# Query and key groups transposed by the DMA engines instead of VectorE

## The chip, the cores and the metric

One core of one Trainium2 chip runs the whole program. The metric is the device time of the program in microseconds (us), the median over runs.

## The reference

Chunked attention (chunks of 64 tokens, each attending only to itself), then a two-layer network with a leaky ReLU. Inputs and output are float32.

```python
batch, n_heads, seq, head_dim = (8, 8, 576, 64)      # q, k, v
chunk = 64
scores = scale * np.matmul(q_c, k_c.transpose(0, 1, 2, 4, 3))     # per chunk of 64
scores = scores - np.max(scores, axis=-1, keepdims=True)
attn = np.exp(scores)
attn = attn / (np.sum(attn, axis=-1, keepdims=True) + 1e-09)
out = np.matmul(attn, v_c)
...
x = out.transpose(0, 2, 1, 3).reshape(4608, 512)
h = x @ w_in                       # 512 x 2048
g = np.maximum(0.01 * h, h)
return g @ w_out                   # 2048 x 512
```

## The kernel before

The 4608 tokens are cut into 36 groups of 128 tokens (two chunks of 64, all eight heads). Each group u goes through the attention stages and leaves 128 columns of `xT`; the network runs over 19 blocks of 128 or 256 tokens. Everything is in float16 on TensorE, with float32 sums.

The order of all instructions is written out by the kernel itself. After a written prologue (`FRONT`), the network's matmuls form a list `chunks`; each of them advances a counter `step` by one (by a half in the last two blocks). Attention stages are events with a due step, `at(step, ...)`, and each is issued when the counter reaches it. `T[u]` is the step at which the scores of group u are due; the distances between neighbours are in the list `SPACE` (3.5 to 10.5 steps). Every engine then executes its own part of that one order, in order.

The stages of a group that matter here:

- loading: `load_qk(u)` (L73) reads q and k of the group by natural rows (token on the partition), float32 in DRAM to float16 in SBUF, by DMAs that GpSimd (POOL) issues (L91), into the tiles `q_in` and `k_in` with five buffers each. For groups 14 to 35 another loader is used: `load_qk_batch` (L95, DMAs at L105) brings one batch of 576 tokens by 16 DMAs, in a layout in which 32x32 blocks can be transposed within 32 partitions (`q_d`, `k_d`).
- transposing: the scores need the head dimension on the partition. For groups below `UD = 14`, TensorE transposes q and k against an identity (`stage_tq`, `stage_tk`, L674) into PSUM (`qp`, `kp`), then VectorE copies q into `QZ` (`stage_q`, L701, two copies a group) and ScalarE copies k into `KT` (`stage_k`, L712). From group 14 on VectorE transposes 32x32 blocks straight into `QZ` (`stage_dq`, L724, two a group) and `KT` (`stage_dk`, L732), 7 steps ahead of the scores.
- scores: `stage_s` (L742), eight matmuls into `Sp`. Then the row maximum `mx` (L751), from group 14 on its negative `nb` (L764) and eight exponentials with row sums on ScalarE (L772); before that a subtraction (L755) and one exponential (L785). The sum with its small addend is `ze` (L796), its reciprocal `zi` (L798), the normalised weights `en` (L803), which VectorE computes for groups below 10 and POOL for the others.
- `stage_d` (L825): one DMA transpose on SyncE's (SP) queue turns `en` into `et`. `stage_v` (L836) multiplies it with v; ScalarE copies the result into `xT` (L850).

v comes by DMAs that POOL issues (L112); one half of a batch's buffer is reloaded when the group that last read it is done. SP's queue also carries all stores of the output (L282 and others).

Below, "group 16" is u = 16, counted from 0, so the tenth group is u = 9.

Of the kernel before, what the change touches and what calls it, by code (L numbers as in the profile page):

```python
# [8 lines left out]
FP16 = mybir.dt.float16  # L9
# [7 lines left out]
def kernel(  # L17
# [9 lines left out]
    nc = tc.nc  # L27

    B, H, S, D = q.shape
# [3 lines left out]
    CH = 64  # L33
# [4 lines left out]
    NQZ = 3  # L38
    NVB = 2
    NIN = 5  # L40
    PAIRED = range(1, 4)
    UD = 14
    LEAD = 5
    UE = 5
    UX = 14
    G = 2 * CH

    NU = n_tok // G
# [9 lines left out]
    sbp = ctx.enter_context(tc.tile_pool(name="k_sb", bufs=1))  # L58
# [5 lines left out]
    QZ = [sbp.tile([128, 4, 2, 2, CH], FP16, name=f"QZ{i}") for i in range(NQZ)]  # L64
# [8 lines left out]
    def load_qk(u):  # L73

        both = []
        for name, src in (("q_in", q), ("k_in", k)):
            if u in PAIRED:
                t = sbp.tile([CH, H, 2, D], FP16, name=name, tag=name + "2", bufs=len(PAIRED))
            else:
                t = sbp.tile([128, H, D], FP16, name=name, tag=name, bufs=NIN)  # L80
            r0, r1 = u * G, (u + 1) * G
            cut = min(-(-r0 // S) * S, r1) if r0 % S else r1
            for a, z in ((r0, cut), (cut, r1)):
                if a < z:
# [7 lines left out]
            both.append(t)  # L92
        qk[u] = tuple(both)

    def load_qk_batch(b, i):  # L95

        if i == 0:
            qkd[b] = tuple(
                sbp.tile([128, 2, 2, S // 32, 32], FP16, name=name, tag=name, bufs=2) for name in ("q_d", "k_d")
            )  # L100
        i, n = divmod(i, 2)
        m, s, dh = i // 4, i // 2 % 2, i % 2
        t, src = qkd[b][n], (q, k)[n]
        p0, h0 = s * 64 + dh * 32, 4 * m + 2 * s
        nc.gpsimd.dma_start(  # L105
            out=t[p0:p0 + 32, m, :, :, :].rearrange("p h b d -> p (h b) d"),
            in_=src[b, h0:h0 + 2, :, dh * 32:dh * 32 + 32].rearrange("h (b t) d -> t (h b) d", t=32),
        )

    def load_v(b):  # L110
        for m in range(2):
            nc.gpsimd.dma_start(  # L112
                out=VB[b % NVB][m * CH:(m + 1) * CH, :, :, m * CH:(m + 1) * CH].rearrange("p h c d -> p (h c) d"),
                in_=v[b, m * H // 2:(m + 1) * H // 2].rearrange("h (c j) d -> j (h c) d", j=CH),
            )
# [21 lines left out]
    for eng, name, src in ((nc.sync, "q_f", q), (nc.scalar, "k_f", k)):  # L137
        t = sbp.tile([128, H, D], FP32, name=name, tag="sh", bufs=2)
# [11 lines left out]
    LOADS = (  # L150
        "g2 g1 g3 v0 Q0 Q1 g4 Q2 Q3 g5 P0 P1 P3 P2 g6 v1 g7 g8 "
    )
    LOADERS = {"g": load_qk, "v": load_v, "Q": load_w_in_quarter, "P": load_w_out_quarter, "D": lambda b: [load_qk_batch(b, i) for i in range(16)]}
    ident = sbp.tile([128, 128], FP16, name="ident")
    for n, what in enumerate(LOADS.split()):
        LOADERS[what[0]](int(what[1:]))
        if n == 0:
# [181 lines left out]
    def w_in_sum(n):  # L339
        h = HF // 2 * 128  # L340
        w = w_inT.rearrange("p (k t) (s h f) -> p k h t s f", k=2, s=2, h=2)
        b11, b12, b21, b22 = w[:, 0, 0], w[:, 0, 1], w[:, 1, 0], w[:, 1, 1]
        x, y = {1: (b12, b11), 2: (b22, None), 3: (b22, b12), 4: (b21, None)}[n]
        if y is None:
            y = WS[{2: 0, 4: 1}[n]]
        to = sbp.tile([128, 2, 2, h], FP16, name=f"WS{n}", tag="q_d" if n % 2 else "k_d", bufs=2, padded_shape=[128, 2, 2, 576])
        for s in range(2):
            nc.vector.tensor_tensor(out=to[:, :, s], in0=x[:, :, s], in1=y[:, :, s], op=ALU.subtract)
        WS.append(to)
# [306 lines left out]
    D_D = 3  # L656
# [35 lines left out]
    def stage_q(u, s, act=0):  # L692
        part = slice(s * CH, (s + 1) * CH)
        to, of = QZ[u % NQZ][part, :, :, s, :], QP[u][part]
        if u in PAIRED:
            to = to.rearrange("p i e (j r) -> p (i e) r j", r=2)
# [4 lines left out]
            nc.vector.tensor_copy(out=to, in_=of)  # L701

    def stage_k(u, dve=0):
        KT[u] = sbp.tile([128, 4, 2, CH], FP16, name="KT", tag="KT", bufs=3)
# [9 lines left out]
    def cuts(u):  # L714
        r0, r1 = u * G, (u + 1) * G
        cut = min(-(-r0 // S) * S, r1) if r0 % S else r1
        return [(a // S, a % S, (a - r0) // CH, (z - a) // CH) for a, z in ((r0, cut), (cut, r1)) if a < z]

    flat = lambda t: t.rearrange("p m h b d -> p (m h) (b d)")

    def stage_dq(u, s):
        qz = QZ[u % NQZ]
        for b, at, e0, n in cuts(u):
            nc.vector.transpose(  # L724
                out=qz[s * CH:(s + 1) * CH, :, e0:e0 + n, s, :],
                in_=flat(qkd[b][0])[s * CH:(s + 1) * CH, :, at:at + n * CH].rearrange("p h (e t) -> p h e t", e=n),
            )

    def stage_dk(u):
        KT[u] = sbp.tile([128, 4, 2, CH], FP16, name="KT", tag="KT", bufs=3)  # L730
        for b, at, e0, n in cuts(u):
            nc.vector.transpose(  # L732
                out=KT[u][:, :, e0:e0 + n, :],
                in_=flat(qkd[b][1])[:, :, at:at + n * CH].rearrange("p h (e t) -> p h e t", e=n),
            )

    def stage_s(u):
        qz, kt = QZ[u % NQZ], KT.pop(u)
# [91 lines left out]
    def stage_v(u):  # L830
        et = ET.pop(u)
        xp = psp.tile([128, NT, 2, CH], FP32, name="xp", tag="ox", bufs=1)
        for e in range(2):
            b, c = divmod(2 * u + e, NCH)
            for t in range(NT):
                nc.tensor.matmul(  # L836
                    out=xp[:, t, e, :],
                    lhsT=VB[b % NVB][:, t, c, :],
                    rhs=et[:, t // 2, e, t % 2, :] if u < UD else et[:, t % 2, e, t // 2, :],
                    start=True,  # L840
                    stop=True,
                )
            if c == NCH - 1 and b + NVB < B:
                load_v(b + NVB)
        XP[u] = xp
# [47 lines left out]
    def zero_act(i):  # L893
# [23 lines left out]
        "I": identity, "st": store_held, "nb": stage_nb, "f": stage_f, "dq": stage_dq, "dk": stage_dk, "D": load_qk_batch,  # L917
# [17 lines left out]
    for what in FRONT.split():  # L935
        name = what.rstrip("0123456789.")
# [8 lines left out]
    VO = [-1.5, 1.0, 0.5, 0.0, 1.0, -0.5, 2.5, 1.5, 0.0, 1.5, 6, 1.5, -0.5, 1.5, -0.5, 1.5, 1.5, -2.5, -0.5, 1.0, 4.5, 0.5, 0.0, 1.0, 3.0, 3.5, -0.5, -1.0, -6.0, -3.0]  # L945
    O_T = 6
    O_P = 4.0
    O_Q = 7.0
    O_R = 1.25
    O_M = 0  # L950
    O_X = 1.5
    O_F = 1.5
# [6 lines left out]
    O_L = 4.0  # L959
    O_W = -13  # L960
    O_Y = 2.5
    O_E = 4
    O_D = 7.5
    T = {6: O_T}
# [5 lines left out]
    for u in range(6, NU):  # L970
        t = T[u]
        if u >= UD:
            at(t - O_Q, "dq", u, 0)
            at(t - O_Q + O_R, "dq", u, 1)
            at(t - O_Q + 2 * O_R, "dk", u)
        elif u > 5:
            for what in ("tq", "tk", "Q", "k"):
                at(t - O_P, what, u)
        at(t, "s", u)
        at(t + O_M, "m", u)  # L980
        if u < UX:
# [12 lines left out]
        at(w, "a", u)  # L994
    for u in range(9, UD):
        at(T[u - 3] - O_D, "g", u)
    for b in range(3, B):
        for i in range(16):
            at(T[9 * b // 2 - 5] - (O_E if b == 3 else O_L) + i // 2 * D_D, "D", b, i)
    for n in range(4):  # L1000
        at(O_W + n * O_Y, "W", n + 1)
    if len(WIDE):
# [49 lines left out]
```

## Time and profile before

| | |
|---|---|
| runs | 280.33, 280.75, 281.57 us; median 280.75 us |
| profiled execution, first to last instruction (span) | 278.6 us |
| outside the span, by the median of the runs | 2.1 us |
| busy: TensorE, weight loads | 271.9 us (98%), 242.6 us (87%) |
| busy: VectorE, ScalarE, GpSimd | 217.2, 202.7, 143.3 us |
| DMA packets, bytes | 182791, 32.66 MB |

The profiled execution's own time is not listed apart from its span; the span is 2.1 us under the median of the runs, and that difference is taken to stay. PE stands for TensorE's matmuls, PEld for its weight loads, DVE for VectorE, ACT for ScalarE, POOL for GpSimd, SP for SyncE. The matmuls' ends in the trace are modelled and overlap, so the time that a matmul costs is read from the starts of neighbours.

### The profile page before, as it was taken

Reading aid. Unit: us, or ns where it says so; the run is one execution under the profiler, and the core shown is the slowest. Engines: PE = TensorE matmul, PEld = TensorE weight load, DVE = VectorE, ACT = ScalarE, POOL = GpSimd, SP = SyncE. Lnnn points to the kernel's source line nnn. Section 1 sums busy time; section 2 is a strip of 40 time slices with the busy share of each in tenths; the row PEclk is TensorE's granted clock in tenths of the full one; section 3 lists DMA queues with packets and bytes.
Section 4 is the critical chain, followed back from the end, with each engine's and each line's share of the span. In section 5 each row is a group of like instructions: output and inputs, shape, how many; then the busy total and the mean of one; then the engine's idle time right before and its main releaser. Section 6 shows DMA issues by size and latency. Waiting matters only on the chain.

```text
span 278.6 us, 8310 instructions
## 1 busy us (share of the span) xinstructions
PE 271.9 (98%) x3320; PEld 242.6 (87%) x3320; DVE 217.2 (78%) x440; ACT 202.7 (73%) x652; POOL 143.3 (51%) x170
## 2 busy tenths in 40 slices
PE   8799999999999999999999999999999999999995
PEld 4479958999999899999999999999998999899994
DVE  5786699899887979797967796858694867777694
ACT  6776724775658787879896978887888888567671
POOL 8848647867576695896569547935120211000000
PEclk9999999999999999999999999999999999999999
DMA  9999999999999999999999999999730513121113
GB/s 144 154 190 189 206 175 157 150 119 111 84 123 149 72 79 145 131 167 80 177 88 141 83 159 224 218 114 147 54 111 6 96 22 94 21 75 40 41 38 115
DMA packets 182791, 32.66 MB, mean 117 GB/s; under 512 B 173792, under 2 KB 178272, under 8 KB 182752
## 3 DMA queue, kind: packets, MB, share of 16 engines
q0 software_dynamic: 158880, 18.23, 131.6%
q1 hardware_dynamic: 22832, 13.64, 22.1%
q8 instruction: 26, 0.43, 0.7%
q10 hardware_dynamic: 1040, 0.26, 0.4%
q14 instruction: 13, 0.11, 0.2%
HBM read 36.96 MB, written 9.44 MB: 167 GB/s over the span
## 4 chain that ended last, share of the span: by engine, by line
PE 91%; DMA 5%; POOL 2%; issue 1%; DVE 0%; POOLq 0%
PE hT L308 39%; PE prX L219 21%; PE prZ L219 7%; PE pr L219 6%; PE prW L219 3%; PE xp L836 3%; DMA VB<-in_v_dram 3%; PE Sp L742 3%; PE xbank L388 3%; PE oP L428 2%; DMA k_in<-in_k_dram 2%; PE xpr L388 2%; PE kp L674 1%; POOL k_in L91 1%; PE qp L674 1%; POOL q_in L91 1%
## 5 line engine op out<-in xcount | busy, mean ns | idle before, releaser
L308 PE MATMUL hT<-xT,w_inT 128*128 128x256 f16 (+1 forms) x1280 | 127.1, 251 | 0.3 <-DMA w_inT<-in_moe_w_in_dram 0.3
L308 PEld LDWEIGHTS <-w_inT 128*128 128x128 f16 x1280 | 102.6, 98 | 8.9 <-issue 0.5
L323 ACT ACTIVATE gT<-hT 128x512 f16<-128x512 f32 x128 | 77.2, 625 | 22.9 <-PE hT L308 22.6
L803 POOL TENSOR_TENSOR en<-ex,zi 128x512 f16<-128x512 f16 x26 | 28.1, 1079 | 60.0 <-DVE zi L798 31.0
L219 PEld LDWEIGHTS <-SG 128*128 128x128 f16 x544 | 51.9, 98 | 5.7
L772 ACT ACTIVATE ex<-Sp,nb 128x64 f16<-128x64 f32 x176 | 52.7, 333 | 3.2 <-DVE nb L764 3.2
L219 PEld LDWEIGHTS <-gT 128*128 128x128 f16 x400 | 37.9, 98 | 4.2
L772 ACT ACTIVATION_READ_ACCUMULATOR ex<-Sp,nb 128x1 f32 x176 | 39.9, 227 | 0.0
L751 DVE TENSOR_REDUCE mx<-Sp 128x8 f32<-128x512 f32 x36 | 24.8, 688 | 18.4 <-PE Sp L742 18.2
L105 POOL DMA_DIRECT2D q_d<-in_q_dram x40 | 33.4, 834 | 5.8 <-DVE QZ L724 5.0
L249 ACT ACTIVATE keep<-prX 128x256 f32<-128x256 f32 x51 | 20.3, 399 | 20.7 <-PE prX L219 20.6
L219 PE MATMUL prX<-TW,SG 128*128 128x256 f16 x272 | 35.3, 273 | 0.0
L105 POOL DMA_DIRECT2D k_d<-in_k_dram x40 | 32.6, 814 | 2.4 <-DVE KT L732 1.4
L724 DVE STREAM_TRANSPOSE QZ<-q_d 64x512 f16<-64x512 f16 (+1 forms) x48 | 31.0, 653 | 0.5
L193 DVE TENSOR_TENSOR SG<-gT 128x1024 f16<-128x1024 f16 x34 | 26.7, 785 | 0.3 <-ACT gT L323 0.2
L850 ACT ACTIVATE xT<-xp 128x512 f16<-128x512 f32 x36 | 22.5, 625 | 4.3 <-PE xp L836 4.3
L112 POOL DMA_DIRECT2D VB<-in_v_dram x16 | 18.5, 1167 | 7.2 <-PE xp L836 7.2
L219 PE MATMUL prX<-w_outT,gT 128*128 128x256 f16 x136 | 17.6, 273 | 0.0
L219 PE MATMUL prX<-TW,gT 128*128 128x256 f16 x128 | 16.6, 273 | 0.0
L91 POOL DMA_DIRECT2D q_in<-in_q_dram x15 | 12.2, 819 | 7.1 <-DMA w_outT<-in_moe_w_out_dram 2.7
L732 DVE STREAM_TRANSPOSE KT<-k_d 128x512 f16<-128x512 f16 (+1 forms) x24 | 15.6, 655 | 0.3
L91 POOL DMA_DIRECT2D k_in<-in_k_dram x15 | 11.9, 792 | 7.7 <-DMA VB<-in_v_dram 4.1
(90 smaller groups left out, 381.1 us busy)
## 6 DMA issues: line engine op xcount, KB each, us to landing
out_dram<-osb SPq DMA_DIRECT2D x35, 256.0 KB, 3.4
VB<-in_v_dram POOLq DMA_DIRECT2D x16, 288.0 KB, 7.5
q_d<-in_q_dram POOLq DMA_DIRECT2D x40, 72.0 KB, 5.2
k_d<-in_k_dram POOLq DMA_DIRECT2D x40, 72.0 KB, 5.1
w_inT<-in_moe_w_in_dram POOLq DMA_DIRECT2D x8, 256.0 KB, 7.4
w_outT<-in_moe_w_out_dram POOLq DMA_DIRECT2D x4, 512.0 KB, 11.2
q_in<-in_q_dram POOLq DMA_DIRECT2D x11, 128.0 KB, 8.5
k_in<-in_k_dram POOLq DMA_DIRECT2D x11, 128.0 KB, 8.2
```

Source lines behind the costliest of these rows:

```text
L91: nc.gpsimd.dma_start(out=to, in_=rows)
L105: nc.gpsimd.dma_start(out=t[p0:p0 + 32, m, :, :, :].rearrange("p h b d -> p (h b) d"), in_=src[b, h0:h0 + 2, :, dh * 32:dh * 32 + 32].rear ...
L193: nc.vector.tensor_tensor(out=SG[j, n], in0=x, in1=y, op=op)
L219: nc.tensor.matmul(out=to[:, i, :], lhsT=left[:, f, i * 128:(i + 1) * 128], rhs=right[:, f, :], start=(j, where) not in opened, stop=(f == ...
L249: nc.scalar.activation(out=half(kept[j, n]), in_=half(bank[j, "X"]), func=AFT.Copy, bias=0.0, scale=1.0)
L308: nc.tensor.matmul(out=hT[:, i, :], lhsT=w_inT[:, t, fc * 128:(fc + 1) * 128], rhs=xT[:, t, r0:r0 + tb], start=(t == 0), stop=(t == NT - 1),)
L323: nc.scalar.activation(out=gT[j][:, nf * a:nf * a + nf, c0:c0 + tb], in_=HT.pop((j, a, p)), func=AFT.Prelu, bias=0.0, scale=1.0, alpha=0.01,)
L724: nc.vector.transpose(out=qz[s * CH:(s + 1) * CH, :, e0:e0 + n, s, :], in_=flat(qkd[b][0])[s * CH:(s + 1) * CH, :, at:at + n * CH].rearran ...
L751: nc.vector.tensor_reduce(out=MX[u], in_=SP[u], axis=AXL.X, op=ALU.max)
L772: nc.scalar.activation(out=E[u][:, i, :], in_=SP[u][:, i, :], func=AFT.Exp, bias=NB[u][:, i:i + 1], scale=SCL, accum_out=Z[u][:, i:i + 1],)
L803: (nc.gpsimd if u >= UP else nc.vector).tensor_tensor(out=E[u], in0=ex, in1=ZI.pop(u).unsqueeze(2).to_broadcast((128, 8, CH)), op=ALU.mult)
L850: nc.scalar.activation(out=xT[:, :, at:at + G], in_=xp, func=AFT.Copy, bias=0.0, scale=1.0)
```

## The change

From group 9 on, q and k are loaded by natural rows, as the groups before are, and two DMA transposes a group on SP's queue (`stage_tdk`, `stage_tdq`) write `KT` and a new tile `QT`, 18 steps ahead of the scores (`O_Q = 18`). Two VectorE copies a group (`stage_cq`) bring `QT` into `QZ`, 2.5 steps ahead of the scores (`O_C = 2.5`). The loads are due 7.5 steps ahead of the transposes (`O_D`). The batch loader, the VectorE transposes, and for groups 9 to 13 the TensorE transposes with their copies, are gone. `KT` has four buffers instead of three, `QT` three. The four tiles `WS` of the last blocks, which had shared the buffers of `q_d` and `k_d`, have buffers of their own, and the order of heads inside `et` is now the same for all groups.

```diff
+    NKT = 4
+    NQT = 3
-    UD = 14
+    UD = 9
...
-    def load_qk_batch(b, i):
...
-        nc.gpsimd.dma_start(
-            out=t[p0:p0 + 32, m, :, :, :].rearrange("p h b d -> p (h b) d"),
-            in_=src[b, h0:h0 + 2, :, dh * 32:dh * 32 + 32].rearrange("h (b t) d -> t (h b) d", t=32),
-        )
...
-        to = sbp.tile([128, 2, 2, h], FP16, name=f"WS{n}", tag="q_d" if n % 2 else "k_d", bufs=2, padded_shape=[128, 2, 2, 576])
+        to = sbp.tile([128, 2, 2, h], FP16, name=f"WS{n}", tag="WS", bufs=4)
...
-    def stage_dq(u, s):
...
-            nc.vector.transpose(
-                out=qz[s * CH:(s + 1) * CH, :, e0:e0 + n, s, :],
...
-    def stage_dk(u):
...
+    def stage_tdk(u):
+        KT[u] = sbp.tile([128, 4, 2, CH], FP16, name="KT", tag="KT", bufs=NKT)
+        nc.sync.dma_start_transpose(
+            out=KT[u].rearrange("p i e c -> p i (e c)"), in_=qk[u][1].rearrange("p h d -> p (h d)")
+        )
+
+    def stage_tdq(u):
+        QT[u] = sbp.tile([128, 4, 2, CH], FP16, name="QT", tag="QT", bufs=NQT)
+        nc.sync.dma_start_transpose(
+            out=QT[u].rearrange("p i e c -> p i (e c)"), in_=qk[u][0].rearrange("p h d -> p (h d)")
+        )
+
+    def stage_cq(u, s):
+        part = slice(s * CH, (s + 1) * CH)
+        nc.vector.tensor_copy(out=QZ[u % NQZ][part, :, :, s, :], in_=QT[u][part])
...
-                    rhs=et[:, t // 2, e, t % 2, :] if u < UD else et[:, t % 2, e, t // 2, :],
+                    rhs=et[:, t // 2, e, t % 2, :],
...
-    O_Q = 7.0
+    O_Q = 18.0
     O_R = 1.25
+    O_C = 2.5
...
         if u >= UD:
-            at(t - O_Q, "dq", u, 0)
-            at(t - O_Q + O_R, "dq", u, 1)
-            at(t - O_Q + 2 * O_R, "dk", u)
+            at(t - O_Q, "tdk", u)
+            at(t - O_Q + O_R, "tdq", u)
+            at(t - O_C, "cq", u, 0)
+            at(t - O_C, "cq", u, 1)
...
-    for u in range(9, UD):
-        at(T[u - 3] - O_D, "g", u)
-    for b in range(3, B):
-        for i in range(16):
-            at(T[9 * b // 2 - 5] - (O_E if b == 3 else O_L) + i // 2 * D_D, "D", b, i)
+    for u in range(9, NU):
+        at((T[u - 3] if u < UD else T[u] - O_Q) - O_D, "g", u)
```

More of the change, by code (lines that the diff above doesn't have):

```diff
@@ L93, in load_qk @@
         qk[u] = tuple(both)
-    def load_qk_batch(b, i):
-        if i == 0:
-            qkd[b] = tuple(
-                sbp.tile([128, 2, 2, S // 32, 32], FP16, name=name, tag=name, bufs=2) for name in ("q_d", "k_d")
-            )
[L101 to L105, printed above, removed]
-            out=t[p0:p0 + 32, m, :, :, :].rearrange("p h b d -> p (h b) d"),
-            in_=src[b, h0:h0 + 2, :, dh * 32:dh * 32 + 32].rearrange("h (b t) d -> t (h b) d", t=32),
-        )
     def load_v(b):
@@ L152 @@
     )
-    LOADERS = {"g": load_qk, "v": load_v, "Q": load_w_in_quarter, "P": load_w_out_quarter, "D": lambda b: [load_qk_batch(b, i) for i in range(16)]}
+    LOADERS = {"g": load_qk, "v": load_v, "Q": load_w_in_quarter, "P": load_w_out_quarter, }
     ident = sbp.tile([128, 128], FP16, name="ident")
@@ L703, in stage_k @@
     def stage_k(u, dve=0):
-        KT[u] = sbp.tile([128, 4, 2, CH], FP16, name="KT", tag="KT", bufs=3)
+        KT[u] = sbp.tile([128, 4, 2, CH], FP16, name="KT", tag="KT", bufs=NKT)
         to, of = KT[u], KP.pop(u)
@@ L712, in stage_k @@
             nc.scalar.activation(out=to, in_=of, func=AFT.Copy, bias=0.0, scale=1.0)
[L714 to L719, printed above, removed]
-    def stage_dq(u, s):
-        qz = QZ[u % NQZ]
-        for b, at, e0, n in cuts(u):
-            nc.vector.transpose(
-                out=qz[s * CH:(s + 1) * CH, :, e0:e0 + n, s, :],
-                in_=flat(qkd[b][0])[s * CH:(s + 1) * CH, :, at:at + n * CH].rearrange("p h (e t) -> p h e t", e=n),
-            )
-    def stage_dk(u):
[L730 to L735, printed above, removed]
+    QT: dict[int, bass.AP] = {}
+    def stage_tdk(u):
+        KT[u] = sbp.tile([128, 4, 2, CH], FP16, name="KT", tag="KT", bufs=NKT)
+        nc.sync.dma_start_transpose(
[9 more added lines that the diff above has]
+        nc.vector.tensor_copy(out=QZ[u % NQZ][part, :, :, s, :], in_=QT[u][part])
     def stage_s(u):
@@ L916 @@
         "A": first_layer, "H": first_act, "S": first_sum, "G": act1, "B": second_layer, "O": finish, "i": idle, "y": zero, "w": zero_act,
-        "I": identity, "st": store_held, "nb": stage_nb, "f": stage_f, "dq": stage_dq, "dk": stage_dk, "D": load_qk_batch,
+        "I": identity, "st": store_held, "nb": stage_nb, "f": stage_f, "tdk": stage_tdk, "tdq": stage_tdq, "cq": stage_cq,
         "WS": w_in_sum, "xs": x_sums, "lx": wide_x, "la": wide_m, "lp": leaky,
```

## The prediction, as it was put on record

> **What bounds the kernel now.** I read the page first, then the busy times by stretch, then TensorE's rows in order of time.
>
> ```profile
> PE 271.9 (98%) x3320; PEld 242.6 (87%) x3320; DVE 217.2 (78%) x440; ACT 202.7 (73%) x652; POOL 143.3 (51%) x170
> PE 91%; DMA 5%; POOL 2%; issue 1%; DVE 0%; POOLq 0%
> 25.00:100.00 75.00, 75.00 (x1031) 67.54 (x1029) 64.10 (x129) 47.51 (x107) 50.34 (x59) 1.00 2.18 133
> 100.00:240.00 140.00, 140.00 (x1531) 126.49 (x1530) 109.22 (x223) 114.94 (x475) 74.12 (x82) 1.00 1.61 117
> ```
>
> The second line is the chain of work that ended last: TensorE holds 91% of the span. The other two are stretches; behind the length stand the busy times of PE, PEld, DVE, ACT and POOL and the granted clock, which is 1.00. From 25 to 240 us TensorE has no gap. So in the region that the change touches, time is the sum of TensorE's instructions. Work taken off VectorE (DVE) or GpSimd (POOL) gains nothing there by itself; work taken off TensorE gains its full length; any new wait of TensorE costs its full length. A wait is not made good later: TensorE has no slack, and the stages behind a late group are released late with it.
>
> **What leaves TensorE.** A comparison of the two programs' instruction orders shows one difference on TensorE: 20 transposes into `qp` and 20 into `kp` go, those of groups 9 to 13. All else stands in the same order.
>
> ```profile
> 54.05 0.39 PE L674 MATMUL qp<-ident,q_in 128*128 128x128 f16 x4
> 54.27 0.39 PE L674 MATMUL kp<-ident,k_in 128*128 128x128 f16 x4
> 54.49 0.27 PE L308 MATMUL hT<-xT,w_inT 128*128 128x128 f16 x2
> ```
>
> Durations overlap, so I take starts: four transposes last 0.22 us, a group's eight 0.44 us (54.49 - 54.05). Five groups: 5 x 0.44 = **2.2 us gained**. It is the only part that shortens the bounding engine.
>
> **What leaves and joins the other engines.**
>
> ```profile
> L724 DVE STREAM_TRANSPOSE QZ<-q_d 64x512 f16<-64x512 f16 (+1 forms) x48 | 31.0, 653 | 0.5
> L724 DVE STREAM_TRANSPOSE QZ<-q_d 64x512 f16<-64x512 f16 x40 | 28.0, 700 | 0.5
> L724 DVE STREAM_TRANSPOSE QZ<-q_d 64x256 f16<-64x256 f16 x8 | 3.1, 417 | 0.0
> L732 DVE STREAM_TRANSPOSE KT<-k_d 128x512 f16<-128x512 f16 (+1 forms) x24 | 15.6, 655 | 0.3
> L701 DVE COPY QZ<-qp 64x512 f16<-64x512 f16 x20 | 8.7, 433 | 2.1 <-PE qp L674 1.9
> L105 POOL DMA_DIRECT2D q_d<-in_q_dram x40 | 33.4, 834 | 5.8 <-DVE QZ L724 5.0 <-DMA q_in<-in_q_dram 0.5 <-DMA q_d<-in_q_dram 0.3
> L105 POOL DMA_DIRECT2D k_d<-in_k_dram x40 | 32.6, 814 | 2.4 <-DVE KT L732 1.4 <-DMA k_in<-in_k_dram 0.8 <-issue 0.2
> L91 POOL DMA_DIRECT2D q_in<-in_q_dram x15 | 12.2, 819 | 7.1 <-DMA w_outT<-in_moe_w_out_dram 2.7 <-issue 1.3 <-POOLq L1036 0.8
> ```
>
> VectorE loses 31.0 + 15.6 us of transposes and ten copies from PSUM (10 x 0.433). It gains 54 copies of the same shape from SBUF, an operation that the trace does not show. The nearest row, L701, has the same shape from PSUM: 0.433 us. From below: half the elements save a transpose 0.700 - 0.417 = 0.283 us, so some 0.13 us are paid whatever the size, and a copy can't be under that. I use 0.43 us, a pair 0.86 us, and keep 0.13 as the low end. Either way VectorE's load falls, by 46.6 + 4.3 - 23 = 28 us at 0.433. POOL drops 80 issues (66 us) and adds 48 (22 groups x 2, two of them cut at a batch's edge) x 0.82 = 39 us. ScalarE drops five copies into `KT`. All of it lies beside TensorE: gain nothing, except room.
>
> **The queues.** SP's queue gets 54 more transposes, and each group's attention weights (`et`) go through the same queue. So each `et` now stands behind a tdk and tdq, which wait for loads.
>
> ```profile
> L825 SPq DMA_TRANSPOSE et<-en x30: 1189/1197/1337, 53.6 to 236.8; - x30
> DMA to landing us min/median/max: 2.4/4.6/7.5
> q_d<-in_q_dram POOLq DMA_DIRECT2D x40, 72.0 KB, 5.2
> 53.61 1.32 SPq L825 DMA_TRANSPOSE et<-en  x1
> et<-en SPq DMA_TRANSPOSE x1, 7.3
> 60.05 1.04 PE L219 MATMUL prX<-TW,SG 128*128 128x256 f16 x8
> 60.97 0.39 PE L836 MATMUL xp<-et,VB 128*128 128x64 f16 x8
> 41.47 0.88 POOL L91 DMA_DIRECT2D k_in<-in_k_dram  x1
> k_in<-in_k_dram POOLq DMA_DIRECT2D x1, 128.0 KB, 8.5
> ```
>
> A transpose holds SP 1.2 us; 84 of them make 101 us of 278.6, so SP is not full. The tight place is group 6, the first `et` on SP: issued at 53.61, landed 7.3 us later at 60.9, used at 60.97. Ahead of it now stand tdk and tdq of group 9. Their load (the 41.47 row) lands at 50.0, so SP is through with them at 50.0 + 2 x 1.2 = 52.4, before `en` of group 6 is ready. Their bytes however are ahead of `et` in the same rings while the loads still fill them. Bounds: nothing, as the batch loads that competed at 53 to 61 are gone; or two more transposes' worth of the shortest landing, 2 x 2.4 = 4.8 us. I take 0.1: the removed loads and the added transposes are of the same size here (two transposes are 0.25 MB, the first four batch DMAs 0.29 MB). For q and k themselves: a step is eight matmuls, 0.9 us (60.05 to 60.97), so tdk and tdq are due some 16 us ahead of the scores, against a landing of at most 7.5 us, and their loads 7.5 steps, 7 us, ahead of them, against landings of about 8 us; a load that is late by a few us shifts SP, not TensorE.
>
> **The copies into QZ.** They are due 2.5 steps ahead of the scores, where the transposes stood 7 steps ahead and the copies from PSUM 4. VectorE executes in order, and what stands ahead of the copies can be a chain that waits. The places where I find it late, in the order of the changed program, are these:
>
> ```profile
> 67.09 0.63 ACT L785 ACTIVATE ex<-sh 128x512 f16<-128x512 f32 x1
> 67.24 0.85 DVE L701 COPY QZ<-qp 64x512 f16<-64x512 f16 x2
> 68.12 0.69 DVE L794 TENSOR_REDUCE z<-ex 128x8 f32<-128x512 f16 x1
> 69.44 0.69 DVE L803 TENSOR_TENSOR en<-ex,zi 128x512 f16<-128x512 f16 x1
> 70.53 0.40 PE L742 MATMUL Sp<-KT,QZ 128*128 128x64 f16 x8
> 102.42 0.82 DVE L796 TENSOR_SCALAR ze<-z 128x8 f32<-128x8 f32 x1 [0.36 <-ACT ex L772]
> 103.70 0.20 DVE L798 RECIPROCAL zi<-ze 128x8 f32<-128x8 f32 x1 [0.47 <-DVE ze L796]
> 104.42 0.40 PE L742 MATMUL Sp<-KT,QZ 128*128 128x64 f16 x8
> 111.18 0.20 DVE L798 RECIPROCAL zi<-ze 128x8 f32<-128x8 f32 x1
> 111.00 0.40 PE L742 MATMUL Sp<-KT,QZ 128*128 128x64 f16 x8
> 129.00 0.20 DVE L798 RECIPROCAL zi<-ze 128x8 f32<-128x8 f32 x1
> 129.86 0.40 PE L742 MATMUL Sp<-KT,QZ 128*128 128x64 f16 x8
> ```
>
> Group 10: its copies now stand behind `en` of group 9, which ended at 70.13 (69.44 + 0.69). Without the copies at 67.24 the sum `z` can start when `ex` ends, 67.72 instead of 68.12, so `en` ends at 69.73 and the pair at 70.59. The scores, at 70.53 before, are due 0.88 us earlier because two groups' transposes are gone ahead of them: 69.65. That is 0.94 us late; as half of the 0.88 also moves the chain's own start, 0.5 is the other end, and I take 0.7. Group 16: behind `zi` of group 15, 103.90 + 0.86 = 104.76 against 104.42: 0.3 us late. Group 17: `zi` ended at 111.38, after the scores at 111.00; but two transposes of `QZ` and one of `KT` (2.1 us) leave the stretch before it, so 109.3 if VectorE alone set it, later if the exponentials do: I take 0.3. Group 20: 129.20 + 0.86 = 130.06 against 129.86: 0.2. In the other groups what stands ahead ends early enough, or ends earlier by the transposes taken out. Sum 0.7 + 0.3 + 0.3 + 0.2 = **1.5 us lost**. With a copy of 0.13 us a pair is 0.6 us shorter, only group 10 is late, by 0.1 at most: 0.1 us. With every late place at its worst (0.94, 0.35, 1.2, 0.2) it is 2.7 us.
>
> Sum: -2.2 + 1.5 + 0.1 = -0.6 us on the span of 278.6 us, so 278.0. Around the span lie 280.75 - 278.6 = 2.1 us, which I keep: **280.2 us**. A change under 0.5% (1.4 us) is about what a measurement of this kernel can't tell from none.
>
> **Rivals.**
>
> *All hidden* (27%): the copies are short, or ScalarE's relief moves the chains ahead, and nothing is late. Then -2.2 to -1.4 us, 278.5 to 279.3; take 278.7. For it: VectorE loses 28 us or more. Against it: group 10's chain is short of 0.9 us only partly for lack of VectorE time.
>
> *Copies held up by POOL* (20%): a stretch in which VectorE and POOL both work in SBUF.
>
> ```profile
> 102.08 2.31 POOL L112 DMA_DIRECT2D VB<-in_v_dram  x2
> 104.38 1.08 POOL L803 TENSOR_TENSOR en<-ex,zi 128x512 f16<-128x512 f16 x1
> 104.16 1.85 DVE L193 TENSOR_TENSOR SG<-gT 128x1024 f16<-128x1024 f16 x1
> L193 DVE TENSOR_TENSOR SG<-gT x34: 639/682/1855, 38.6 to 271.4; 128x1024 f16<-128x1024 f16 x34
> ```
>
> The sum `SG` took 1.85 us where its median is 0.68, while `en` ran on POOL, and it ended 0.6 us after that; `ze` above, a tiny operation, took 0.82 us and ended with the first half of the `VB` issue. So some VectorE operations wait out a whole POOL instruction. If the new copies are such, the second of a pair falls behind `en`, released by the same `zi`, at groups 16, 17 and 20: 3 x (1.08 - 0.3 of margin) = 2.3 us, and a load issue of 0.82 us stands in the way at one or two more groups, 1.0 us. Lost 1.5 + 2.3 + 1.0 = 4.8 us, less 2.2: +2.6 us, 283.3. It decides once a copy's end moves by more than 1 us in three groups. The Trainium skill (SBUF — State Buffer, "Who interferes with whom") says that VectorE and GpSimd share a port pair as an exclusive lock, that copies in a two-port mode take it, and that the later one blocks fully; the `SG` row agrees, and by that rule the copies are exposed while the removed transposes were not.
>
> *Queue of transposes* (11%): `et` comes late because three transposes a group share the rings with POOL's loads. At group 6, 4.8 us at most, at groups 7 to 10 less; -0.6 + 2 to 4.8 gives 282.2 to 285, take 283.5. The rows speak for it only where the loads are thick: 7.3 us to landing at 53.6, and the share of 2.18 in the stretch to 100 us. Against it: a transposed 128x512 tile can land in 2.4 us. The Trainium skill (VectorE: DVE Perf Modes, "The three transpose paths") prices a 128x128 DMA transpose at 1309 ns; four of these in a row would be 5.2 us a tile and 15.7 us a group, more than a group's distance. The 2.4 us row disagrees, so I give that no chance of its own.
>
> That the change does not do what it says is excluded by the order: the transposes are gone from TensorE.
>
> **How the numbers follow.** Forecast, some copies late: 42%, -1.4 to +1.0 us, 279.3 to 281.7. Faster by over 0.5%: all hidden, 0.27, and the forecast's low edge, 0.02: 0.29. Slower by over 0.5%: the two slow rivals, 0.31, and 0.02 of the forecast: 0.33. The rest, 0.38, is within 0.5%. The range goes from everything hidden (278.5, with 0.2 of scatter) to just past the two slow rivals' own values, 283.6, which leaves out a little over one in ten above.
>
> **What would show it.** In the changed profile the starts around the scores of groups 9 to 13 should be 0.44 us closer per group; TensorE should wait on L717 (the copies) at groups 10, 16, 17 and 20 for 0.2 to 0.7 us, and at no `xp`. Copies of 1 us or more next to POOL's `en` show the port rival; waits of `xp` on `et` show the queue rival; a `KT` that TensorE waits for would show that 18 steps are too few. No wait at all, and the forecast was too high by 1.5 us.

## The result, and the profile after

The changed kernel is slower: 287.56 us median (four runs, 287.09 to 292.67) against 281.11 us in runs beside it, ratio 1.0228, 95% interval 1.0204 to 1.0252. The predicted 280.2 us is too low, and the range, to 283.6 us, ends below the result too. The profiled execution took 287.09 us, 285.3 us of it the span: 6.7 us more than before. Runs over 1.5% above the fastest of the same kernel are in the medians but not in the ratios: the 292.67 us here, and below one run each of e2, e3 and e4 and two of e7, the profiled one among these.

From the page of the changed kernel: busy times, the two DMA queues that matter (queue: packets, MB, share of 16 engines' time) and the chain that ended last; then, from its view of the DMAs, the transposes with the median time to landing. Queue q0 carries the loads that POOL issues, in packets of some 160 bytes; q1 carries SP's transposes and stores. "Rings" below means these queues on the 16 DMA engines.

```profile
PE 272.2 (95%) x3280; PEld 240.3 (84%) x3280; DVE 191.1 (67%) x412; ACT 200.7 (70%) x647; POOL 120.2 (42%) x138
q0 software_dynamic: 111264, 18.09, 93.3%
q1 hardware_dynamic: 52208, 20.72, 46.7%
PE 61%; DMA 21%; DVE 7%; SPq 3%; ACT 2%; POOL 2%; issue 2%; DVEq 0%; ACTq 0%; POOLq 0%
et<-en SPq DMA_TRANSPOSE x30, 5.7
KT<-k_in SPq DMA_TRANSPOSE x27, 5.4
QT<-q_in SPq DMA_TRANSPOSE x27, 5.7
```

What the change says it does, it does: TensorE has 40 matmuls fewer, VectorE 26 us and POOL 23 us less work. But TensorE's share of the chain fell from 91% to 61%, and DMA's rose from 5% to 21%. The median landing of `et` went from 4.6 to 5.7 us.

The same two stretches as before (length, then busy time of PE, PEld, DVE, ACT, POOL, granted clock, DMA share, GB/s), and what TensorE and VectorE waited for (total us, times, longest):

```profile
25.00:100.00 75.00, 72.44 (x984) 64.45 (x982) 61.32 (x125) 44.30 (x97) 37.31 (x41) 1.00 1.83 150
100.00:240.00 140.00, 136.39 (x1478) 121.27 (x1477) 80.44 (x190) 111.70 (x464) 63.10 (x67) 1.00 1.59 156
```

```profile
PE xp L818 <- DMA et<-en: 4.0, 5, 1.2
PE Sp L724 <- DVE QZ L717: 1.9, 5, 0.6
DVE QZ L717 <- DMA QT<-q_in: 11.0, 6, 3.2
POOL q_in L93 <- DMA QT<-q_in: 9.7, 1, 9.7
```

TensorE, without a gap before, is idle 2.56 + 3.61 us in them. Line 818 is `xp`, which waits for `et`; line 724 the scores, which wait for the copies into `QZ` (L717). The idle time understates the waits, since records of matmuls overlap. I therefore count a wait as the distance between the starts of two neighbouring matmuls less the median distance for that operation and shape, and add all above 15 ns after 25 us. That gives 0.05 us for the kernel before and 8.2 us for the changed one: 4.8 us of `xp` on `et` (groups 8, 10, 11, 20, 28: 0.73, 1.10, 1.22, 1.37, 0.43) and 3.4 us of scores on copies (groups 17, 19, 20, 25, 28, 29, 30 with 0.27 to 0.73, and 0.08 at group 10). With the saving, 278.6 - 2.2 + 8.2 = 284.6, against a measured span of 285.3 us. These two kinds of wait are the loss.

At groups 10, 11, 20 and 28 SP issued `et` 1.3 to 2.7 us after `en` was ready, behind transposes of q and k; at group 8 it issued `et` at once, and `et` landed 8.1 us later, behind a pair of transposes that had gone out just before.

One late `et`, of group 20, in the timeline of the changed kernel (start us, length, engine, line; in brackets the idle time before it and what ended it), and then the two transfers issued between 140.0 and 140.2 us, with their time to landing:

```profile
135.47 1.85 SPq L705 DMA_TRANSPOSE KT<-k_in  x1
137.18 1.32 POOL L785 TENSOR_TENSOR en<-ex,zi 128x512 f16<-128x512 f16 x1 [0.74 <-ACT gT L310]
137.42 2.54 SPq L711 DMA_TRANSPOSE QT<-q_in  x1
138.45 0.94 POOL L93 DMA_DIRECT2D q_in<-in_q_dram  x1
139.38 0.88 POOL L93 DMA_DIRECT2D k_in<-in_k_dram  x1
140.06 1.28 SPq L807 DMA_TRANSPOSE et<-en  x1
...
150.51 0.41 PE L818 MATMUL xp<-et,VB 128*128 128x64 f16 x8 [1.21 <-DMA et<-en]
```

```profile
k_in<-in_k_dram POOLq DMA_DIRECT2D x1, 128.0 KB, 11.2
et<-en SPq DMA_TRANSPOSE x1, 10.4
```

`en` is ready at 138.50, but SP is still issuing the transposes of group 23, and the issue of QT takes 2.54 us instead of 1.2. `et` goes out 1.56 us late, behind two transposes, while POOL has just put two more loads on the rings; it lands 10.4 us after its issue, at 150.46. TensorE starts `xp` 0.05 us later, having stood idle 1.21 us.

### The profile page after: what moved, and what is told of

Its sections match the earlier page's. It is cut to its first block, busy times and chain, and to the rows that moved or that the text cites. A ratio compares the mean times of both kernels' runs of the same rounds, so it can differ in the third digit from the quotient of the medians.

```text
span 285.3 us, 8309 instructions
## 1 busy us (share of the span) xinstructions
PE 272.2 (95%) x3280; PEld 240.3 (84%) x3280; DVE 191.1 (67%) x412; ACT 200.7 (70%) x647; POOL 120.2 (42%) x138
## 3 DMA queue, kind: packets, MB, share of 16 engines
q0 software_dynamic: 111264, 18.09, 93.3%
## 4 chain that ended last, share of the span: by engine, by line
PE 61%; DMA 21%; DVE 7%; SPq 3%; ACT 2%; POOL 2%; issue 2%; DVEq 0%; ACTq 0%; POOLq 0%
PE hT L295 24%; PE prX L206 14%; DMA et<-en 12%; PE prZ L206 5%; PE pr L206 4%; DMA QT<-q_in 4%; DMA VB<-in_v_dram 3%; DVE QZ L717 3%; PE xbank L375 3%; PE prW L206 2%; PE oP L415 2%; DMA k_in<-in_k_dram 2%; PE Sp L724 2%; PE xp L818 2%; PE xpr L375 2%
## 5 line engine op out<-in xcount | busy, mean ns | idle before, releaser
L93 POOL DMA_DIRECT2D q_in<-in_q_dram x39 | 33.7, 868 | 15.1 <-DMA QT<-q_in 9.7
L93 POOL DMA_DIRECT2D k_in<-in_k_dram x39 | 32.7, 843 | 6.6 <-DMA w_outT<-in_moe_w_out_dram 3.4
L717 DVE COPY QZ<-QT 64x512 f16<-64x512 f16 x54 | 23.8, 440 | 11.4 <-DMA QT<-q_in 11.0
L180 DVE TENSOR_TENSOR SG<-gT 128x1024 f16<-128x1024 f16 x34 | 25.1, 737 | 0.3 <-ACT gT L310 0.3
L778 DVE TENSOR_SCALAR ze<-z 128x8 f32<-128x8 f32 x36 | 8.1, 225 | 18.9 <-ACT ex L754 18.3
L257 DVE TENSOR_TENSOR osb<-prZ,keep 128x256 f32<-128x256 f32 x22 | 9.4, 429 | 13.6 <-ACT keep L236 9.6
L818 PE MATMUL xp<-et,VB 128*128 128x64 f16 x288 | 14.3, 193 | 4.0 <-DMA et<-en 4.0
L818 PEld LDWEIGHTS <-VB 128*128 128x128 f16 x288 | 12.9, 98 | 5.8 <-DMA et<-en 3.6
```

The source lines that it names most:

```text
L93: nc.gpsimd.dma_start(out=to, in_=rows)
L180: nc.vector.tensor_tensor(out=SG[j, n], in0=x, in1=y, op=op)
L717: nc.vector.tensor_copy(out=QZ[u % NQZ][part, :, :, s, :], in_=QT[u][part])
L818: nc.tensor.matmul(out=xp[:, t, e, :], lhsT=VB[b % NVB][:, t, c, :], rhs=et[:, t // 2, e, t % 2, :], start=True, stop=True,)
```

## The experiments

Theories at the start: **Queue** (the transposes of q and k stand ahead of `et` on SP and share the rings with POOL's loads), **Place** (the copies stand right ahead of their scores, behind late chains or held up by POOL), and **Load** (the natural loads alone). The table gathers the runs: the waits counted as above, the span worked out as 278.6 - 2.2 + waits (without the 2.2 where TensorE keeps its transposes), the measured span of the profiled execution, the median of the runs and the ratio to the kernel before in runs beside it. "Ahead" is counted in steps, of some 0.9 us each. "Other" are matmuls that wait for loads of weights, q or k before 35 us, later for VectorE, mostly its sums, and in e2, e4 and e7 also matmuls at a lower clock (last section).

| kernel | `xp` on `et` | scores | other | span worked out | span | median | ratio [95%] |
|---|---|---|---|---|---|---|---|
| changed | 4.8 | 3.4 | 0 | 284.6 | 285.3 | 287.56 | 1.0228 [1.0204, 1.0252] |
| e1 no transposes of q, k | 0.7 | 2.3 | 1.1 | 280.5 | 281.7 | 281.23 | 1.0021 [0.9996, 1.0046] |
| e6 e1, copies 6.0 ahead | 0.4 | 0.5 | 1.1 | 278.4 | 279.7 | 279.57 | 0.9955 [0.9937, 0.9973] |
| e2 before + 54 transposes | 8.5 | 7.1 | 9.5 | 303.7 | 304.6 | 305.46 | 1.0806 [1.0747, 1.0865] |
| e3 `et` first | 0.4 | 4.9 | 0 | 281.7 | 281.5 | 284.51 | 1.0115 [1.0071, 1.0160] |
| e10 e3, loads earlier | 0.4 | 4.2 | 0.7 | 281.6 | 282.5 | 284.29 | 1.0112 [1.0063, 1.0160] |
| e11 e10, a group further ahead | 2.2 | 2.1 | 0.6 | 281.2 | 281.2 | 283.85 | 1.0100 [1.0059, 1.0141] |
| e12 e11, copies 4.0 ahead | 2.8 | 0.3 | 2.1 | 281.6 | 281.8 | 282.24 | 1.0052 [1.0022, 1.0082] |
| e13 e11, copies 6.0 ahead | 1.6 | 0.1 | 4.3 | 282.4 | 282.8 | 285.22 | 1.0142 [1.0099, 1.0185] |
| e4 changed, copies 6.0 ahead | 7.7 | 0.7 | 4.5 | 289.3 | 288.5 | 291.94 | 1.0383 [1.0328, 1.0437] |
| e5 changed, loads earlier | 2.5 | 4.1 | 0.4 | 283.4 | 284.8 | 284.22 | 1.0138 [1.0089, 1.0187] |
| e7 e3, copies and loads earlier | 0.3 | 4.3 | 18.4 | 299.4 | 300.0 | 299.75 | 1.0574 [1.0481, 1.0666] |
| e8 before, `UD` = 9 | 0 | 1.4 | 3.8 | 281.7 | 281.5 | 283.25 | 1.0101 [1.0068, 1.0134] |
| e9 changed, `UD` = 14 | 1.7 | 2.6 | 0 | 282.9 | 283.0 | 285.56 | 1.0171 [1.0111, 1.0232] |

In every row the working holds to 1.4 us: these waits make the time, with a slower TensorE only in e2, e4 and e7, where the matmuls at a lower clock are counted in. The profile is one execution, and those of e1 and e6 are the longest of their ten runs (283.66 and 281.69 us); runs of these kernels scatter by several us, so rows closer than that are compared by their medians.

**e1: without the transposes.**

```diff
-        nc.sync.dma_start_transpose(out=KT[u]..., in_=qk[u][1]...)
+        KT[u] = still["k"]        # a zero tile, set once; QT likewise
```

> Leaves out the two DMA transposes a group: from group 9 on the scores read tiles of zeros that are set once; the loads by natural rows, the copies into QZ and all other work stay. Theory 'queue' (the transposes of q and k on SP's queue and in the DMA rings make et late, and QT late for some copies): the waits of xp on et go from 4.8 us to under 0.5 us, those of the copies for QT vanish, and the time falls from 287.6 to 281 to 282 us. Rival 'loads' (the natural-row loads by themselves crowd the rings): the waits of xp stay at 3 us or more and the time stays above 285. Rival 'copies' (the copies are late by their own place): the waits of the scores on the copies stay at 1.5 to 3.4 us here too; this run says how much of 3.4 us that is.

Measured 281.23 us. By the ratios, 2.1% or 5.8 us of the changed kernel's time is gone. The landing of `et`, and the waits of TensorE:

```profile
et<-en SPq DMA_TRANSPOSE x30, 4.3
```

```profile
PE Sp L725 <- DVE QZ L718: 1.4, 3, 0.6
PE xp L819 <- DMA et<-en: 0.6, 1, 0.6
```

`et` lands in 4.3 us again, so the 54 transposes, and not the natural loads alone, made it late. Load falls, as far as this run can say: nothing reads the loads here, so their buffers come free at once. The waits on `et` of the changed kernel are all gone; the 0.7 us in the table stands at group 6. What stays, 2.3 us, is Place: the scores of groups 10, 12, 17, 20 and 25 wait 0.08, 0.63, 0.30, 0.73 and 0.56 us though `QT` is never late (late chain or POOL: see the section on the prediction).

**e6: the same with the copies earlier.**

```diff
-    O_C = 2.5
+    O_C = 6.0
```

> Leaves out the two DMA transposes a group, as the run without them did (zeros in place of transposed q and k), and has the copies due 6 steps ahead instead of 2.5. With nothing to wait for, only the copies' place is left. Theory 'copies late by their place': the 2.3 us of waits of the scores vanish and the full 2.2 us of TensorE's saving shows: 279 us. Rival 'blocked by POOL's port wherever they stand': waits stay over 1.5 us, 281.

Measured 279.57 us, 0.45% under the kernel before and, by the ratios, 0.7% or 1.8 us under e1, with 0.5 us left at the scores. That is Place's price, and it shows that the saving on TensorE is real. It leaves the transposes out, so it is no kernel to use.

**e2: the transposes added to the kernel before.**

```diff
+    def stage_xt(u, n):
+        to = sbp.tile([128, 4, 128], FP16, name="xto", tag=f"xto{n}", bufs=2)
+        nc.sync.dma_start_transpose(out=to, in_=w_inT[:, 0, :512])
...
+        if u >= 9:
+            at(t - 18.0, "xt", u, 0)
+            at(t - 18.0 + O_R, "xt", u, 1)
```

> The kernel before, with 54 DMA transposes added on SP's queue at the steps at which the change has its own, from a weight slice that is long loaded into tiles that nobody reads. They wait for no load and no compute result. Theory 'queue by bytes' (the transposes' own traffic ahead of et in the rings delays et): xp waits on et by 3 to 5 us, 281.1 becomes 284 to 286. Rival 'queue by waits' (SP stands still for loads that have not landed, and et behind it): et is late by little, under 1.5 us in all, 281 to 282.5.

Measured 305.46 us, 8% slower, though nothing reads these transposes and they wait for no load. The DMA issues of that run:

```profile
q_d<-in_q_dram POOLq DMA_DIRECT2D x40, 72.0 KB, 9.2
k_d<-in_k_dram POOLq DMA_DIRECT2D x40, 72.0 KB, 9.8
xto<-w_inT SPq DMA_TRANSPOSE x54, 7.1
et<-en SPq DMA_TRANSPOSE x30, 6.9
```

The batch loads, 5.2 and 5.1 us in the kernel before, land in 9.2 and 9.8, and `et` in 6.9 instead of 4.6. So it isn't only the order on SP: the transposes delay the loads, though they go out on another queue. The trace of the changed kernel speaks for a delay the other way too: 12 of its 84 transposes are in flight while q0 moves nothing, and they land in 2.5 us at the median (2.4 to 4.1); the other 72 land in 6.1 us (2.9 to 10.4). In e2 VectorE waited 9.9 us for late `q_d`, and TensorE 7.1 us at the scores behind it. The changed kernel pays less than this; it also drops 80 batch loads, and the packets on q0 fall to 111264 from the 158880 of this run.

**e3: `et` first.**

```diff
-            at(t - O_Q, "tdk", u)
-            at(t - O_Q + O_R, "tdq", u)
...
         for what in ("z", "n", "d"):
             at(n, what, u)
+        if UD <= u + 3 < NU:
+            at(n, "tdk", u + 3)
+            at(n, "tdq", u + 3)
```

> The changed kernel, but the two transposes of group u + 3 stand on SP's queue right behind the et transpose of group u, so that nothing of them stands between et and its issue. Theory 'queue': the waits of xp fall from 4.8 to under 1.5 us and the time by 3 to 4 us to about 284. Rival 'rings crowded by the loads': et still lands 8 us after its issue at groups 8, 10, 11, 20, and the time stays within 1 us of 287.6. The copies' lateness (3.4 us) stays in both.

Measured 284.51 us: half of the loss is gone with as many transposes as before. TensorE's waits on `et` fall from 4.8 to 0.4 us, so the order on SP decided those: the median landing of `et` is still 5.6 us, but its issue no longer stands behind a pair of transposes of q and k. The waits of scores rise to 4.9 us; 1.8 us of it stands at group 12, whose `QT` landed at 80.2 us, 0.9 us ahead of its scores at 81.1. VectorE waited 16.1 us for `QT`, off TensorE's path for the most part:

```profile
PE Sp L724 <- DVE QZ L717: 2.5, 3, 1.6
DVE QZ L717 <- DMA QT<-q_in: 16.1, 9, 3.0
```

**e5 and e10: earlier loads**, without and with `et` first.

```diff
-    O_D = 7.5
+    O_D = 14.0
-    NIN = 5
+    NIN = 6
```

> The changed kernel with the loads of q and k due 14 steps ahead of their transposes instead of 7.5, and six input buffers instead of five. Theory 'SP stands still for loads' (77 us of SP's idle time is put down to k_in): tdk and tdq no longer wait, et is issued on time, the waits of xp fall from 4.8 to under 2 us and the time to about 284. Rival 'rings': et is issued on time but still lands 7 to 8 us later behind the other transposes' bytes, xp waits stay over 3 us, 286 to 288.

> The changed kernel with the transposes of group u + 3 issued right behind et of group u, and with the loads 14 us instead of 7.5 us ahead of their transposes and six instead of five buffers for them; the copies stay at 2.5 us ahead of the scores. If what was left of the loss with et first (3.7 us above the kernel before) is QT landing late because its load was late, the waits of Sp fall from 4.9 us to the 2.3 us that remain without any transposes, and the time to about 281.5 to 282 us. If the transposes and the loads share rings that are full whatever the order (the loads' packets are the same number, only earlier), QT stays late at the same groups and the time stays at 284 to 285 us.

Measured 284.22 and 284.29 us. Alone, the earlier loads win 0.9% by the ratios, 2.5 us, not much less than `et` first; the two together win no more. What SP waited for at L705 (the transposes of k), in the changed kernel and then in e5:

```profile
SPq L705 <- DMA k_in<-in_k_dram: 77.2, 10, 48.8
```

```profile
SPq L705 <- DMA k_in<-in_k_dram: 52.5, 2, 50.4
```

Without the one long wait at the start, that is 28.4 us in the changed kernel and 2.1 us in e5: SP stood still for late loads, and `et` stood behind. Of the 2.5 us on `et` that e5 has left, 1.7 us stand at group 6, which did not wait in the changed kernel. In e10 `QT` still came late at some groups: group 12's transpose was issued at 73.8 us and landed at 80.8, and its scores waited 0.9 us.

**e11: a group further ahead.** The transposes of group u + 4 behind `et` of group u, `NQT` = 4, loads at 14.0 with five input buffers again.

```diff
-        if UD <= u + 3 < NU:
-            at(n, "tdk", u + 3)
-            at(n, "tdq", u + 3)
+        if u == 6:
+            at(n, "tdk", 9)
+            at(n, "tdq", 9)
+        if UD < u + 4 < NU:
+            at(n, "tdk", u + 4)
+            at(n, "tdq", u + 4)
```

> As the run with et first, but each group's transposes one group further ahead (group u + 4 behind et of group u, from the eleventh group on), with four instead of three buffers for QT and the loads 14 us ahead; five buffers for the loads. If lateness of QT alone is left, a group more (6.5 us) covers landings of 5 to 10 us, VectorE never waits for QT, and the time is 281 to 282 us, with Sp waits of some 2.3 us from the copies' place. If the rings' total traffic is what costs (loads landing later, et landing in 6 to 8 us), it stays at 284 us or goes up, since the loads then wait for buffers.

Measured 283.85 us. VectorE never waits for `QT`; at the scores 2.1 us are left, as in e1. But `et` of group 8, now behind two more transposes, is 1.96 us late.

**e4 and e7: earlier copies without earlier transposes.** `O_C` = 6.0 in the changed kernel, and in e3 with loads 12 steps ahead and six buffers.

> The changed kernel with the copies into QZ due 6 steps ahead of the scores instead of 2.5. Theory 'copies late by their place and by POOL's port': the waits of the scores fall from 3.4 us to under 1 us, what is left being groups whose QT has not landed (19, 28, 29), and the time by 2 to 3 us to 285. Rival 'QT lands late': the copies wait for QT on VectorE instead, hold up its queue, and the time is the same or longer.

> Everything that was found to help, together: the transposes of q and k right behind et, loads due 12 steps ahead with six buffers, copies due 6 steps ahead. Theory 'order and due times': waits of xp and of the scores both under 1 us, 280 to 281. Rival 'the DMA engines themselves are full': QT still lands late, the copies hold VectorE up, 283 or more.

Measured 291.94 and 299.75 us. A copy that waits for a DMA stops VectorE, which works in order. VectorE waited 26.2 us for `QT` in e4 (longest 6.3) and 34.4 us in e7, and TensorE then waited for VectorE's sums (in e4 more for `et`, 7.7 us):

```profile
PE pr L206 <- DVE SG L180: 6.1, 2, 3.1
PE prX L206 <- DVE SG L180: 4.4, 2, 3.5
```

These are e7's.

**e12 and e13: both mended.** As e11, but three groups ahead up to group 11, and the copies 4.0 or 6.0 steps ahead.

```diff
+        for w in (u + 3,) if u < 8 else (u + 3, u + 4) if u == 8 else (u + 4,):
+            if UD <= w < NU:
+                at(n, "tdk", w)
+                at(n, "tdq", w)
...
-    O_C = 2.5
+    O_C = 4.0
```

> The transposes four groups ahead behind et (three groups ahead up to group 11, so that et of group 8 has only one pair ahead of it), loads 14 us ahead, four buffers for QT, and the copies 4.0 us instead of 2.5 us ahead of the scores. If late et and late copies are the whole loss, the profiled 2.1 us of Sp waits and 2.0 us of xp at group 8 of the run four groups ahead go, at most 1 us is left, and the time is the kernel before less 2.2 us plus 1 us, 279 to 280 us: faster than before by some 0.4%. If all kernels with 54 transposes share a third cost, the waits go down and the time stays at 283 to 284 us. If the earlier copies hold VectorE up behind QT as they did with the copies 6 us ahead in the changed kernel, waits on VectorE's products of 2 us and more appear and the time is 285 us or more.

> As the run with the copies 4.0 us ahead, with 6.0 us. By the landing of QT in the run four groups ahead (64.0 us for group 9, 70.9 us for group 11, 117.3 us for group 19, 182.2 us for group 29, against copies that began at 64.1, 72.5, 120.7 and 186.8 us and would now begin some 3.5 us earlier) VectorE waits 3.4 us at group 9 and 1.9 us at group 11 and little elsewhere. If these waits have cover, as late-copy theory needs, the time is that of the copies at 4.0 us or lower, 279 to 280 us; if not, 282 us and more, with TensorE waiting for VectorE's drains (products, SG) around 61 to 73 us.

Measured 282.24 and 285.22 us. With 4.0, scores wait 0.3 us in all: Place and late `QT` are gone, and the time is the best of the kernels that do all the work, but 0.5% over the kernel before. What is left is Queue again, at other places: group 27's `xp` came 1.95 us late and group 11's 0.88, each started within 0.14 us of the landing of its `et`; 2.1 us stand elsewhere (0.8 at 25 us at a matmul that waits for its network weights from DRAM, 1.1 at sums of VectorE). At group 27 the view of waits names a copy of ScalarE that ended in the same moment; that copy reads `prX`, which is not a tile that `xp` needs. The expected 279 to 280 us was too low: I had counted the old places of waiting as gone without asking which `et` was next with no slack. No third cost is needed: the sum gives 281.6 against a span of 281.8 us. With 6.0, VectorE waits 5.1 us for `QT`, about as much as expected, and that has no cover: TensorE stands 2.2 and 0.8 us for its sums at 65.5 and 82.1 us. No version that does all the work beats the kernel before.

**e8 and e9: which groups.** The kernel before with VectorE transposes from group 9 on (`UD` = 9, the third batch loaded by its batch loader too), and the changed kernel with `UD` = 14.

> The kernel before, but VectorE's transposes begin at group 9 instead of 14: one more batch comes by the batch loader, and the 40 TensorE transposes go as in the change, with no DMA transpose added. If the 2.2 us on TensorE can be had without SP's queue: 278.9. If the batch lands too late behind the weights (it is due for group 9 at about 58 us): a wait of the scores at groups 9 and 10 and 280 to 284.

> The changed kernel with natural loads and DMA transposes from the fifteenth group on (UD = 14) instead of the tenth, so that TensorE keeps its 40 transposes of groups 9 to 13 and 44 of the 54 DMA transposes stay. If the slots of TensorE before et (groups 10 and 11: 2.3 us of the 4.8 us of waits on et) come from the first ten transposes, and each group after the fourteenth costs what it cost before, the late part alone remains: waits of some 5.5 us and no saving, so 286 us. If the harm were mostly that of the early groups, where TensorE transposes, natural loads and the batch loads overlap, it would fall to 282 to 283 us. If the early groups had paid for themselves (a saving of 2.2 us against less waiting), it would be slower than the change, 288 us or more.

Measured 283.25 and 285.56 us. The two stretches of e8, then those of e9:

```profile
25.00:100.00 75.00, 71.16 (x956) 62.16 (x954) 67.45 (x130) 41.15 (x93) 51.47 (x59) 1.00 2.09 129
100.00:240.00 140.00, 140.00 (x1537) 126.49 (x1535) 105.98 (x225) 116.19 (x480) 76.33 (x84) 1.00 1.57 117
```

```profile
25.00:100.00 75.00, 75.00 (x1030) 67.54 (x1028) 61.88 (x126) 47.56 (x109) 37.15 (x40) 1.00 1.62 134
100.00:240.00 140.00, 136.69 (x1491) 122.18 (x1489) 81.15 (x192) 112.41 (x469) 63.16 (x67) 1.00 1.52 155
```

TensorE's gaps are in the early stretch alone in e8 (5.3 us of waits, mostly on VectorE, against 2.2 saved) and in the late one alone in e9 (4.3 us, nothing saved). So the early groups, where the saving lies, cost more than they save with VectorE transposes; and in the late groups, where TensorE had nothing to win, DMA transposes only cost. In the changed kernel the waits of the early groups are 3.1 us and those from group 17 on 5.1 us.

## Why the prediction was wrong

**TensorE's saving: right.** 40 transposes, 2.2 us: with it the sums of the table hold, and e6 shows it as time. It is smaller than either kind of wait.

**The queues: the step that failed.** The term was 0.1 us for `et`; it measured 4.8 us, and none of these waits is left without the transposes (e1). Three parts of the step were wrong. It checked group 6, the place named tight, where no wait appeared, and took the later groups as having room; the waits came at groups 8, 10, 11, 20 and 28. (Group 6 had no room either: it waited 0.7 us in e1 and 1.7 us in e5.) It weighed the transposes' bytes against the removed batch loads' near group 6 only. And "a load that is late by a few us shifts SP, not TensorE" overlooked that `et` is behind on that same SP: at group 20, 1.56 us of issue and a landing of 10.4 us. The rival *Queue of transposes*, given 11% and 283.5 us, was the right mechanism with too small a size: it scaled the shortest landing, 2.4 us, which holds where no load is in flight, and looked for the crowd only up to group 10. KT and QT landed in 5.4 and 5.7 us at the median, but that is a time shared with others: the landing of `et` moves from 4.3 (e1) to 6.9 us (e2) with what else is in the rings. The 5.2 us a tile that the prediction worked out from the Trainium skill (VectorE: DVE Perf Modes, "The three transpose paths") and set aside is near these medians; the traces bear out that size for crowded rings, and not as a price of the transpose alone, since tiles landed in 2.4 us too.

**The copies: right in place, too small, and mostly another mechanism.** The term was 1.5 us at groups 10, 16, 17 and 20, for copies behind late chains. Without the transposes it is 2.3 us (e1); group 17 came out as forecast (0.3), group 20 at 0.73 instead of 0.2, group 10 at 0.08 instead of 0.7, group 16 at none, and groups 12 and 25 (0.63, 0.56) were not foreseen. Another 1.1 us in the changed kernel is `QT` landing late, at groups 19, 28 and 29, where the copies start within 0.03 us of its landing; the prediction had excluded that by 18 steps of lead. The copy's price of 0.43 us is near the mean, 0.440 us, but that mean mixes two kinds: the median is 0.291 us, and copies beside POOL take up to 2.00 us. The copies of the changed kernel (durations in ns, min/median/max, then busy us and mean ns), and those of group 20 in its timeline:

```profile
L717 DVE COPY QZ<-QT x54: 233/291/2000, 63.7 to 233.9; 64x512 f16<-64x512 f16 x54
L717 DVE COPY QZ<-QT 64x512 f16<-64x512 f16 x54 | 23.8, 440 | 11.4 <-DMA QT<-q_in 11.0
```

```profile
130.65 0.20 DVE L780 RECIPROCAL zi<-ze 128x8 f32<-128x8 f32 x1
130.77 1.41 DVE L717 COPY QZ<-QT 64x512 f16<-64x512 f16 x2
131.00 1.04 POOL L785 TENSOR_TENSOR en<-ex,zi 128x512 f16<-128x512 f16 x1 [3.16 <-ACT gT L310]
```

A pair takes 0.58 us by itself and 1.41 us here, ending 0.14 us after `en`. The pairs of groups 12, 17, 20 and 25 in e1, where the scores wait:

```profile
81.55 1.41 DVE L718 COPY QZ<-QT_still 64x512 f16<-64x512 f16 x2
111.28 1.41 DVE L718 COPY QZ<-QT_still 64x512 f16<-64x512 f16 x2
130.88 1.41 DVE L718 COPY QZ<-QT_still 64x512 f16<-64x512 f16 x2
162.64 2.25 DVE L718 COPY QZ<-QT_still 64x512 f16<-64x512 f16 x2
```

Each lost 0.83 us or more beside POOL's `en` (group 25 beside a load of `VB` too), more than its scores waited. By this estimate some 2.2 of the 2.3 us are POOL's doing, and late chains are left with the 0.08 us of group 10; in the changed kernel groups 17, 20 and 25 are of this kind, 1.6 us, and group 30, another 0.6 us, in part (its pair took 0.85 us). The 0.3 us at group 17 was therefore right by luck. So *Copies held up by POOL* (20%) had the mechanism of the copies: the second of a pair falls behind `en`. The port lock that the prediction cited from the Trainium skill (SBUF — State Buffer, "Who interferes with whom") agrees with these rows. Its 283.3 us was nearer than the forecast, for a part of the loss. Moved ahead (e12), the copies cost 0.3 us.

**All hidden** is out. **What would show it** named waits of `xp` on `et` as the sign of the queue rival, and that is what the profile shows.

**Settled and open.** Shown by leaving out, adding and reordering: the transposes make `et` and `QT` late, through SP's order and through the shared rings. Worked out from durations, and not shown by a run of its own: that POOL's work makes the copies late; e6 and e12 moved the copies and left POOL's work in place. How the rings divide time between a transpose and a load with small packets was not measured by itself.

## What to carry to other kernels

Before a transfer is put on a queue, list what else on that queue has no slack, and price the newcomer by landings in the stretch where it will run, not by the fastest one in the trace. Work taken off an engine with time to spare buys nothing: here VectorE lost 26 us and GpSimd 23 us of work, only the 2.2 us taken off TensorE counted, and the DMA engines that took the work on were the ones feeding TensorE's next step. When one waiting place is mended, look for the next transfer with the least slack before counting the gain.

## What the runs showed of the hardware that was not expected

TensorE can pay twice for a long wait. In e4 it waited 3.89 us for `et` of group 28, and the clock was down after that. The timeline, and then stretches with the granted clock third from the end:

```profile
207.75 0.58 PE L818 MATMUL xp<-et,VB 128*128 128x64 f16 x8 [3.89 <-DMA et<-en]
208.15 1.89 PE L206 MATMUL prX<-TW,gT 128*128 128x256 f16 x8
```

```profile
202.00:207.50 5.50, 1.86 (x18) 1.52 (x16) 1.18 (x3) 0.38 (x1) 0.00 (x0) 0.98 1.90 144
207.50:211.00 3.50, 3.25 (x23) 2.42 (x23) 0.97 (x5) 3.11 (x18) 0.00 (x0) 0.54 1.62 122
211.00:214.00 3.00, 3.00 (x36) 2.71 (x35) 2.38 (x6) 2.56 (x11) 2.81 (x3) 1.00 0.66 136
```

Eight matmuls took 1.89 us instead of 1.04, and the mean granted clock was 0.54 for 3.5 us: by the starts of the matmuls, 1.4 us more on top of the wait. The Trainium skill (TensorE: Matmul & The Clock Gate, "Part 1: The HAM clock gate") says that an idle window of about 3.4 us drops the array to half rate until a busy window of that length has passed. This wait agrees; other waits show that the idle time before the drop can be shorter and that its length alone does not decide. The clock also fell after 3.10 us of idle time at group 18 in e2 (a mean of 0.50 over the next 4 us) and after 2.51 us at group 31 in e7 (0.59), and it stayed at 1.00 after 2.94 us at group 10 in e2. In the changed kernel the longest of the waits was 1.4 us and the clock stayed at 1.00; in e2 and e7 the drops are part of the time.
